# Two contraction blocks in three split passes, sums with a guard column, and value products one block of work later

## The chip, the cores and the metric

The kernel runs on one core of one Trainium2 chip. The metric is device time in microseconds (us); the median of three runs of the kernel before is 1055.7 us (1055.4 to 1057.94). The engines that matter are PE (matrix products), ACT and DVE (elementwise work, also out of the matrix product's banks), POOL (elementwise work between tiles in SBUF, and some of the transfers) and SP, whose queue starts most transfers.

## What is computed

Chunked attention feeds a first gated layer, and that feeds a second one. Attention has 4 batches, 8 heads, 768 positions and a head size of 64. The keys of a chunk of 32 positions are 8 memory keys, 16 to its left, its own 32 and 8 to its right.

```python
def _attn_ref(q, k, v, mem_k, mem_v) -> np.ndarray:
...
    for c in range(nc):
...
        scores = scale * np.matmul(q_c, k_full.transpose(0, 1, 3, 2))
        scores = scores - np.max(scores, axis=-1, keepdims=True)
        a = np.exp(scores)
        a = a / (np.sum(a, axis=-1, keepdims=True) + 1e-09)
        out[:, :, c_start:c_end] = np.matmul(a, v_full)

def _moe_ref(x, w1, w2, w3, w_out) -> np.ndarray:
    a = x @ w1
    b = x @ w2
    h = a * b @ w3
    return (h @ w_out).astype(np.float32)

def _moe2_ref(x, w_a, w_b, w_out) -> np.ndarray:
    a = x @ w_a
    b = x @ w_b
    return (a * b @ w_out).astype(np.float32)
```

There are 3072 tokens of width 512. The inner width is 1024 in the first layer and 1536 in the second.

## The kernel before

**Order.** The kernel is written under a manual schedule: each engine, and each queue of transfers, takes its instructions in the order in which the program issues them. So the place of a call in the Python loops is its place on the engine.

**The weights' product.** Since `h @ w_out` is `(a * b) @ (w3 @ w_out)`, the kernel first makes the product of `w3` and `w_out` once. This is the tile `wps` (loop at L576 of the profile): two halves, in each half eight contraction blocks k, in each block four banks m, so 64 products of 128 x 128 by 128 x 512 in full fp32. The profile lists each of these as two PE records. A number `g = 2k + m // 2` counts 16 places in a half. Behind a place come one "slot" of attention and, at listed places, `w_tick()`, which moves a three-step pipeline of weight loads by one (scaling on ACT at L403 and L404, joining of the halves of a word on DVE at L409, splitting into high and low parts on ACT and DVE). When the eighth block of a bank is done, `w_evict` (L571) takes it out of its bank: a high part on ACT (L573), and a low part on DVE.

**Split products.** All later matrix products are made from split factors. ACT rounds a factor to fp32r (the high part, `split_hi`, L104), DVE subtracts it from the factor (the low part, `split_lo`, L107), and three passes are summed in one bank: high by high, high by low, low by high.

**Attention.** It is done in 16 units, u = 0 to 15, each with two groups of 96 query rows and 4 head pairs. The stages of a unit are: `a_k`, `a_q`, `a_v` (transfers of keys, queries, values, on SP's queue), `a_scores` (tile `sc`, 96 small products on PE), `a_max` (largest score, and its subtraction, on DVE), `a_exp` (ACT), `a_norm` for each half of the heads (sum, plus 1e-9, reciprocal and multiplication; DVE, and the multiplication of u < 6 on POOL), `a_trans` (tile `pt`, 8 transposes on PE), `a_pt` (copy of `pt` to `p2` on ACT), `a_pv` (tile `xp`, 96 small products with the values on PE) and `a_x` (`xp` into the token tile `xt`, or, for the last two token tiles, over `xo` to DRAM, `xd`). `pt` and `xp` share one pair of banks (tag `px`), and `p2` and `xo` share one buffer (tag `p2`, one buffer).

Each stage has a slot: `BASE[u]` plus an offset, for u > 2 the offsets 8 (transposes and `p2`), 11 (value product and the next unit's values) and 12 (`a_x`); the next unit but one begins 14 slots behind `BASE[u]`, since units lie 7 slots apart. `between()` (L702) is called twice in each step of the first layer, once behind `psA` and once behind `psB` (12 split products of 128 x 512 each), and runs as many slots as a pace needs that is worked out from `NEED`, the slot by which a token tile has to be there.

**Layers.** Token tiles 0 to 3 go through `psA`, `psB` (gate) and `psY` (product with the weights' product) while attention runs beside them. Tiles 4 and 5 and the second layer go through a scheme of seven block products (`ps`, `ops`), which the change doesn't touch.

The pieces of code that matter here, as the profile numbers them:

## Time and profile before

| | us |
|---|---|
| median of the runs | 1055.7 (1055.4 to 1057.94) |
| profiled execution | 1054.13 |
| its span in the trace | 1052.3 |
| PE busy | 1045.2 |
| DVE, ACT, POOL busy | 595.1, 446.5, 250.4 |

The span is what the trace sees from the first to the last instruction; 1.8 us of the profiled execution lie outside it. The granted clock of PE is 1.00 in every slice. A PE row of the timeline is drawn somewhat longer than the distance to the next row's start (records overlap in the pipeline), so the price of a group on PE is read as the distance from its start to the start of what follows.

### The profile page before, as it was taken

The numbers are of one execution on the slowest core, as the hardware profiler recorded it, in microseconds if no ns is written. First come the engines' busy times: TensorE is split into PE (matmuls) and PEld (weight loads), VectorE is DVE, ScalarE is ACT, GpSimd is POOL, SyncE is SP. The second block draws the span as 40 slices with busy tenths as digits, with TensorE's granted clock in tenths as the row PEclk, the third lists the DMA queues.
The fourth block names the chain that finished last, engine by engine and source line by source line (L and its number), as shares of the span: only waits on it lengthen the run. The fifth ranks groups of instructions, "written<-read, shape, count | busy, mean of one in ns | idle before, by whom it ended". The sixth has DMA issues, their size and how long they took to land.

```text
span 1052.3 us, 18316 instructions
## 1 busy us (share of the span) xinstructions
PE 1045.2 (99%) x7394; PEld 835.9 (79%) x7394; DVE 595.1 (57%) x950; ACT 446.5 (42%) x797; POOL 250.4 (24%) x264
## 2 busy tenths in 40 slices
PE   9999999999999999999999999999999999999998
PEld 3458788888888888888888888888888888888886
DVE  5889946766775437257666656554444454444410
ACT  5666623434544434344654445333434334343310
POOL 0102498132222000000133334012232202322210
PEclk9999999999999999999999999999999999999999
DMA  9986567678886333144533332344332323222211
GB/s 331 322 218 196 147 200 261 202 243 285 293 275 189 113 101 101 70 132 130 188 111 116 137 133 70 121 143 153 135 130 71 115 76 111 70 70 71 71 40 40
DMA packets 77301, 157.35 MB, mean 150 GB/s; under 512 B 8224, under 2 KB 38304, under 8 KB 75936
## 3 DMA queue, kind: packets, MB, share of 16 engines
q1 hardware_dynamic: 68944, 123.10, 35.5%
q0 software_dynamic: 8064, 33.03, 9.5%
q8 instruction: 58, 0.95, 0.4%
q14 instruction: 27, 0.22, 0.1%
q10 hardware_dynamic: 208, 0.04, 0.0%
HBM read 118.92 MB, written 37.22 MB: 148 GB/s over the span
## 4 chain that ended last, share of the span: by engine, by line
PE 91%; DMA 4%; DVE 2%; ACT 1%; issue 1%; SPq 0%; DVEq 0%; ACTq 0%
PE ps L913 40%; PE ops L95 19%; PE psY L95 11%; PE psB L95 7%; PE psA L95 7%; PE wps L95 3%; PE xp L95 2%; DMA raw<-in_w3a 2%; PE sc L95 1%; DMA raw<-in_w 1%; PE pt L233 1%; DMA q<-in_qt 1%; DVE dec L409 0%; DMA xb<-yd 0%; ACT raw L403 0%
## 5 line engine op out<-in xcount | busy, mean ns | idle before, releaser
L913 PE MATMUL ps<-x,w 128*128 128x512 f32 x1848 | 425.5, 389 | 0.2 <-ACT tmp L925 0.2
L913 PEld LDWEIGHTS ps<-x,w 128*128 128x128 f32 x1848 | 346.6, 188 | 73.2 <-ACT tmp L925 1.1
L925 ACT ACTIVATE tmp<-ps 128x512 f32<-128x512 f32 x132 | 78.6, 596 | 267.5 <-PE ps L913 245.4
L107 DVE TENSOR_TENSOR w<-w 128x512 fp32r<-128x512 f32 (+1 forms) x176 | 108.0, 631 | 79.7 <-ACT w L104 79.5
L1085 DVE TENSOR_TENSOR tmp<-ps,tmp 128x512 f32<-128x512 f32 x108 | 74.6, 691 | 130.0 <-PE ps L913 96.3
L95 PE MATMUL psY<-g,wo 128*128 128x512 f32 x576 | 134.5, 391 | 0.0
L95 PEld LDWEIGHTS psY<-g,wo 128*128 128x128 f32 x576 | 107.4, 188 | 22.4
L1098 POOL TENSOR_TENSOR g<-tmp,g 128x512 fp32r<-128x512 f32 x66 | 88.8, 1360 | 150.3 <-ACT g L104 150.3
L95 PE MATMUL ops<-wo,g 128*128 128x512 f32 x504 | 118.6, 389 | 0.0
L95 PEld LDWEIGHTS ops<-wo,g 128*128 128x128 f32 x504 | 94.6, 188 | 19.6
L804 POOL DMA_DIRECT2D w<-wc x36 | 20.0, 557 | 354.6 <-PE ps L913 216.5
L95 PE MATMUL psA<-xt,w 128*128 128x512 f32 x384 | 94.5, 395 | 0.3 <-ACT xt L104 0.3
L95 PE MATMUL psB<-xt,w 128*128 128x512 f32 x384 | 93.8, 393 | 0.0
L104 ACT ACTIVATE w<-w 128x512 fp32r<-128x512 f32 (+1 forms) x176 | 92.1, 572 | 1.9 <-DMA w<-wd 1.9
L95 PEld LDWEIGHTS psA<-xt,w 128*128 128x128 f32 x384 | 70.8, 188 | 16.1 <-ACT xt L104 1.1
L95 PEld LDWEIGHTS psB<-xt,w 128*128 128x128 f32 x384 | 71.2, 188 | 15.0
L95 PE MATMUL ops<-fo,g 128*128 128x512 f32 x288 | 68.2, 389 | 0.0
L403 ACT ACTIVATE raw<-raw 128x512 f32<-128x512 f32 (+1 forms) x66 | 49.0, 743 | 33.2 <-DMA raw<-in_wab 17.9
L95 PEld LDWEIGHTS ops<-fo,g 128*128 128x128 f32 x288 | 54.1, 188 | 11.2
L95 PE MATMUL wps<-w_f 128*128 128x512 f32 x128 | 57.6, 599 | 0.7 <-DVE w_f L409 0.7
L104 ACT ACTIVATE g<-tmp 128x512 fp32r<-128x512 f32 x82 | 47.2, 624 | 19.1 <-DVE tmp L929 11.1
L404 ACT ACTIVATE raw<-raw 128x512 uint32<-128x512 uint32 (+1 forms) x66 | 49.0, 742 | 0.0
(73 smaller groups left out, 933.7 us busy)
## 6 DMA issues: line engine op xcount, KB each, us to landing
w<-wc POOLq DMA_DIRECT2D x36, 640.0 KB, 4.2
raw<-in_wab SPq DMA_DIRECT2D x24, 512.0 KB
v<-in_vw SPq DMA_DIRECT2D x64, 168.0 KB
w<-wc POOLq DMA_DIRECT2D x36, 256.0 KB, 3.7
kraw<-in_kt SPq DMA_DIRECT2D x16, 512.0 KB
raw<-in_w3a SPq DMA_DIRECT2D x6, 1024.0 KB
q<-in_qt SPq DMA_DIRECT2D x16, 384.0 KB
wc<-cs SPq DMA_DIRECT2D x12, 512.0 KB
```

What stands on the lines that cost most here:

```text
L95: nc.tensor.matmul(o, lhsT=l, rhs=r, start=first, stop=last)
L104: nc.scalar.activation(hi, src, AF.Copy)
L107: nc.vector.tensor_tensor(lo, src, hi.bitcast(F32), ALU.subtract)
L233: nc.tensor.transpose(pt[:, a // 4, a % 4, :], t[:, a].rearrange("p r k -> p (r k)"), id_sb)
L403: nc.scalar.activation(h, h, AF.Prelu, scale=2.0**-112, alpha=2.0**32)
L404: nc.scalar.activation(l, l, AF.Copy, scale=2.0**-29)
L804: (nc.gpsimd if c else nc.sync).dma_start(out=t[:, 1, :C7].bitcast(F32), in_=wseq[n][:, :C7])
L913: nc.tensor.matmul(ps, lhsT=w[i][:, a, k, :], rhs=xs[i][:, b, k, :], start=first and n == 0, stop=n == 5, skip_group_check=not first,)
L925: nc.scalar.activation(z, ps, AF.Copy)
L1085: nc.vector.tensor_tensor(z, ps, y, ALU.add)
L1098: nc.gpsimd.tensor_tensor(g[:, 1, :], z, g[:, 0, :].bitcast(F32), ALU.subtract)
```

## The change

There are four parts.

1. In the second half of the weights' product the blocks k = 6 and 7 are made from split factors: `w_split` rounds the two factors of a block on ACT and takes the low parts on POOL, and `w_mm` issues three passes in place of one full fp32 product. The new tiles lie in a pool of weight loads whose work is then over (tag `raw2`, three buffers). The turns of `w_tick` at g = 13 and 14 of this half move to 12 and 13.
2. The tile `t` of a unit's exponentials becomes one of two persistent tiles `tt`. A head pair's 128 columns lie there in rows of 129, with a column of 1e-9 at each border, set once by POOL. One reduction over 65 elements (64 keys and a guard column) and one reciprocal per unit replace two reductions, two additions and two reciprocals. The multiplication runs on POOL for u = 0 alone, and otherwise on DVE.
3. From u = 4 on the slots of a unit are 9 (transposes and `p2`), 14 (value product, next values) and 15 (`a_x`) in place of 8, 11 and 12, and `NEED` is 3 slots later.
4. The first keys and queries (`a_k(0)`, `a_q(0)`) are called at g = 2 and 3 of the first half, and no longer at g = 0.

```diff
@@ -35,6 +35,7 @@
 KD = DM // P
 M1 = DF1 // P
 M2 = DF2 // P
+KR = 2 * KEYS + 1
 NEG = -1.0e30
 CH = 512
 BUFS = {"raw64": (3, 0), "raw2": (0, 3), "dec": (4, 3)}
@@ -98,6 +99,7 @@
     ks, qs, scs, soft, pts, p2s, xps = ({} for _ in range(7))
     v = att.tile([P, NE, NC, 4 * D], F32, tag="v", bufs=1, name="v")
     kw = att.tile([P, NH, NC, KEYS], F32, tag="kw", bufs=1, name="kw")
+    tt = [att.tile([GQ, NH * KR + 1], F32, tag="t", bufs=2, name="tt") for _ in range(2)]
     xt = {}
 
     def split_hi(hi, src):
@@ -182,6 +184,11 @@
         m = mask_sb[rs, None, None, 0 : c1 - c0].to_broadcast([CHUNK, 2, 4, c1 - c0])
         nc.vector.tensor_tensor(x, x, m, ALU.add)
 
+    def with_eps(u):
+        t = tt[u % 2]
+        p, x = t.ap
+        return bass.AP(t.tensor, t.offset, [p, [KR * x[0], NH], [(KEYS + 1) * x[0], 2], [x[0], KEYS + 1]])
+
     def a_max(u):
         sc = scs.pop(u)
         for e in range(NE):
@@ -191,7 +198,8 @@
                 a_edge(sc, slice(0, CHUNK), hs, NMEM, NMEM + LEFT)
             if g == NG - 1:
                 a_edge(sc, slice(GQ - CHUNK, GQ), hs, KEYS - RIGHT, KEYS)
-        t = att.tile([GQ, NH, 2, KEYS], F32, tag="t", bufs=2, name="t")
+        t = tt[u % 2][:, : NH * KR].rearrange("p (a x) -> p a x", x=KR)[:, :, 1:]
+        t = t.rearrange("p a (r k) -> p a r k", r=2)
         mx = att.tile([GQ, 2, NH], F32, tag="mx", bufs=2, name="mx")
         sm = att.tile([GQ, NH, 2], F32, tag="sm", bufs=2, name="sm")
         nc.vector.tensor_reduce(mx, sc, axis=mybir.AxisListType.X, op=ALU.max)
@@ -215,11 +223,11 @@
     def a_norm(e):
         def stage_of(u):
             t, mx, sm = soft[u][1:]
+            if e == 0:
+                nc.vector.tensor_reduce(sm, with_eps(u), axis=mybir.AxisListType.X, op=ALU.add)
+                nc.vector.reciprocal(sm, sm)
             t, sm = t[:, 4 * e : 4 * e + 4], sm[:, 4 * e : 4 * e + 4]
-            nc.vector.tensor_reduce(sm, t, axis=mybir.AxisListType.X, op=ALU.add)
-            nc.vector.tensor_scalar_add(sm, sm, 1e-9)
-            nc.vector.reciprocal(sm, sm)
-            (nc.gpsimd if u < 6 else nc.vector).tensor_tensor(
+            (nc.gpsimd if u < 1 else nc.vector).tensor_tensor(
                 t, t, sm[:, :, :, None].to_broadcast([GQ, 4, 2, KEYS]), ALU.mult
             )
 
@@ -292,7 +300,7 @@
         todo.setdefault(s, []).extend(stages)
 
     for u in range(NA):
-        t0, t1, t2, t3 = SLOTS.get(u, (8, 8, 11, 12))
+        t0, t1, t2, t3 = SLOTS.get(u, (8, 8, 11, 12) if u < 4 else (9, 9, 14, 15))
         for s, stage_of in (
             (t0, a_trans),
             (t1, a_pt),
@@ -318,7 +326,7 @@
     NEED = []
     for i in range(NT1):
         u = -(-TT * (i + 1) // (NE * GQ)) - 1
-        NEED.append(BASE[u] + (13 if u > 2 else 10))
+        NEED.append(BASE[u] + (16 if u >= 4 else 13 if u > 2 else 10))
     acount = [0]
 
     held_back = []
@@ -555,8 +563,13 @@
 
     w_load()
     warm = psd.tile([P, 512], F32, tag="d", name="warm")
-    wz = att.tile([GQ, 2, TT], F32, tag="t", bufs=2, name="wz")[:, 0]
+    wz = att.tile([GQ, NE, 4, GQ], F32, tag="p2", bufs=1, name="wz")
+    wz = wz.rearrange("p e a q -> p (e a q)")[:, :TT]
     nc.vector.memset(wz, 0.0)
+    for i in range(2):
+        p, x = tt[i].ap
+        eps = bass.AP(tt[i].tensor, tt[i].offset, [p, [KR * x[0], NH + 1]])
+        nc.gpsimd.memset(eps, 1e-9)
     for _ in range(5):
         mm(warm[:GQ], wz[:, :GQ], wz, True, True)
     w_load()
@@ -573,17 +586,32 @@
         nc.scalar.activation(w[:, 0, :], banks[m], AF.Copy)
         nc.vector.tensor_tensor(w[:, 1, :], banks[m], w[:, 0, :].bitcast(F32), ALU.subtract)
 
+    S3 = (6, 7)
+    w_hl = {}
+
+    def w_split(i):
+        k, j = S3[i // 2], i % 2
+        if k not in w_hl:
+            w_hl[k] = p0.tile([P, 4, CH], F32R, tag="raw2", bufs=3, name="w_hl")
+        x = w3k[8 + k] if j else wo_f[k]
+        h, l = w_hl[k][:, 2 * j], w_hl[k][:, 2 * j + 1]
+        nc.scalar.activation(h, x.bitcast(F32), AF.Copy)
+        nc.gpsimd.tensor_tensor(l, x.bitcast(F32), h.bitcast(F32), ALU.subtract)
+        (wo_f, w3k)[j][(k, 8 + k)[j]] = (h, l)
+
+    def w_mm(o, k, kk, m):
+        a, b = w3k[kk], wo_f[k]
+        if not isinstance(a, tuple):
+            mm(o, a.bitcast(F32)[:, P * m : P * m + P], b.bitcast(F32), k == 0, k == 7)
+            return
+        for i, (p, q) in enumerate(PASSES):
+            mm(o, a[p][:, P * m : P * m + P], b[q], k == 0 and i == 0, k == 7 and i == 2)
+
     for half in range(2):
         banks = [psd.tile([P, 512], F32, tag="d", name="wps") for _ in range(4)]
         for k in range(8):
             for m in range(4):
-                mm(
-                    banks[m],
-                    w3k[8 * half + k].bitcast(F32)[:, P * m : P * m + P],
-                    wo_f[k].bitcast(F32),
-                    k == 0,
-                    k == 7,
-                )
+                w_mm(banks[m], k, 8 * half + k, m)
                 if k == 7 and m > 0:
                     w_evict(half, m - 1)
                 if m % 2 == 0:
@@ -594,8 +622,9 @@
                         attn_slot()
                     if g in (0, 2, 4, 6, 8, 9):
                         w_tick()
-                    if g == 0:
+                    if g == 2:
                         a_k(0)
+                    if g == 3:
                         a_q(0)
                     if g == 7:
                         a_keys(0)
@@ -606,9 +635,12 @@
                         w_turn()
                 else:
                     attn_slot()
+                    for i in range(2 * len(S3)):
+                        if (2, 6, 3, 7, 7, 8, 11, 12)[i] == g:
+                            w_split(i)
                     if g == 0:
                         w_next()
-                    if g in (1, 4, 5, 6, 9, 10, 13, 14):
+                    if g in (1, 4, 5, 6, 9, 10, 12, 13):
                         w_tick()
         w_evict(half, 3)
     del pairs["f"]
```

On PE, in a stretch of the first layer with tiles of later units, the value product of a unit stands by itself before (`psA` and `psB` are the two gate products of a step, `w_...` its weights, `sc` the scores, `pt` the transposes):

```order
L95 MATMUL xp<-p_1884,v 64x32 x48
L95 MATMUL psA<-xt,w_869 128x512 x12
L95 MATMUL psB<-xt,w_869 128x512 x12
L95 MATMUL sc<-kw,q 32x64 x48
L95 MATMUL psA<-xt,w_934 128x512 x12
L233 MATMUL pt<-id_sb,t 128x96 x8
L95 MATMUL psB<-xt,w_934 128x512 x12
```

and in the changed kernel, in the same steps:

```order
L96 MATMUL psA<-xt,w_884 128x512 x12
L96 MATMUL xp<-p_1887,v 64x32 x48
L96 MATMUL sc<-kw,q 32x64 x48
L96 MATMUL psB<-xt,w_884 128x512 x12
L96 MATMUL psA<-xt,w_947 128x512 x12
L241 MATMUL pt<-id_sb,tt 128x96 x8
L96 MATMUL psB<-xt,w_947 128x512 x12
```

The value product now stands directly ahead of the scores of the unit after the next, so that two groups of small products lie in one gap between the large ones instead of two. This is so ten times (value products of u = 4 to 13).

On ACT, in the last blocks of the weights' product's second half (`raw_...` is the scaling of a landed weight block, `p_...` the copy of u = 2's transposes, `w_...` a high part, `wo` the eviction of a bank of the weights' product, `xt` the high part of the first token tile), before:

```order
L445 ACTIVATE w_657<-dec 128x512
L403 ACTIVATE raw_579<-raw_579 128x512
L404 ACTIVATE raw_579<-raw_579 128x512
L239 ACTIVATE p_695<-pt 128x768
L445 ACTIVATE w_699<-dec 128x512
L403 ACTIVATE raw_664<-raw_664 128x512
L404 ACTIVATE raw_664<-raw_664 128x512
L573 ACTIVATE wo<-wps 128x512
L445 ACTIVATE w_699<-dec 128x512
L403 ACTIVATE raw_677<-raw_677 128x512
L404 ACTIVATE raw_677<-raw_677 128x512
L573 ACTIVATE wo<-wps 128x512 x2
```

and in the changed kernel:

```order
L453 ACTIVATE w_656<-dec 128x512
L411 ACTIVATE raw_581<-raw_581 128x512
L412 ACTIVATE raw_581<-raw_581 128x512
L453 ACTIVATE w_697<-dec 128x512
L411 ACTIVATE raw_663<-raw_663 128x512
L412 ACTIVATE raw_663<-raw_663 128x512
L247 ACTIVATE p_712<-pt 128x768
L453 ACTIVATE w_697<-dec 128x512
L411 ACTIVATE raw_676<-raw_676 128x512
L412 ACTIVATE raw_676<-raw_676 128x512
L586 ACTIVATE wo<-wps 128x512 x3
```

The copy of the transposes now stands behind the scaling of one more weight block (raw_663, the block that was raw_664), and the first eviction behind both blocks.

On SP's queue of transfers at the start (`raw_...` are weight blocks, `kraw` and `q` the first keys and queries), before:

```order
L388 DMA raw_154<-in_w3a 128x2048
L388 DMA raw_167<-in_w3a 128x2048
L123 DMA kraw<-in_kt 128x2x512
L130 DMA q<-in_qt 128x2x384
L388 DMA raw_181<-in_w3a 128x2048
L388 DMA raw_192<-in_w3a 128x2048
```

and in the changed kernel:

```order
L396 DMA raw_158<-in_w3a 128x2048
L396 DMA raw_171<-in_w3a 128x2048
L396 DMA raw_181<-in_w3a 128x2048
L125 DMA kraw<-in_kt 128x2x512
L132 DMA q<-in_qt 128x2x384
L396 DMA raw_196<-in_w3a 128x2048
```

The seventh weight block now goes ahead of the first keys and queries.

## Rows read from the trace of the kernel before

**Rows 1.** The page, part 1: busy us, share of span, instructions.

```profile
PE 1045.2 (99%) x7394; PEld 835.9 (79%) x7394; DVE 595.1 (57%) x950; ACT 446.5 (42%) x797; POOL 250.4 (24%) x264
```

**Rows 2.** Waits of PE: us in total, times, longest us.

```profile
PE wps L95 <- DVE w_f L409: 0.7, 2, 0.5
PE psA L95 <- ACT xt L104: 0.3, 1, 0.3
PE pt L233 <- DVE xt L107: 0.3, 1, 0.3
```

**Rows 3.** Chain that ended last, in order of time: start us, us, what.

```profile
18.04 8.89 DMA raw<-in_w3a
30.95 9.16 DMA q<-in_qt
41.44 5.35 PE wps L95 x12
```

**Rows 4.** Timeline of PE, 163 to 185: start, us, what [wait <- releaser].

```profile
163.88 2.88 PE L95 MATMUL psA<-xt,w 128*128 128x512 f32 x12
166.60 2.88 PE L95 MATMUL psB<-xt,w 128*128 128x512 f32 x12
169.41 1.60 PE L95 MATMUL xp<-p,v 64*64 64x32 f32 x96
170.95 3.02 PE L95 MATMUL psA<-xt,w 128*128 128x512 f32 x12
173.80 2.88 PE L95 MATMUL psB<-xt,w 128*128 128x512 f32 x12
176.62 1.20 PE L95 MATMUL sc<-kw,q 64*32 64x64 f32 x96
177.74 3.02 PE L95 MATMUL psA<-xt,w 128*128 128x512 f32 x12
180.60 0.82 PE L233 MATMUL pt<-id_sb,t 96*128 96x96 f32 x8
181.21 3.01 PE L95 MATMUL psB<-xt,w 128*128 128x512 f32 x12
```

**Rows 5.** Timeline of PE, 219 to 232, scores directly ahead of transposes.

```profile
219.69 1.20 PE L95 MATMUL sc<-kw,q 64*32 64x64 f32 x96
220.81 0.88 PE L233 MATMUL pt<-id_sb,t 96*128 96x96 f32 x8
221.48 8.45 PE L95 MATMUL psY<-g,wo 128*128 128x512 f32 x36
229.85 1.60 PE L95 MATMUL xp<-p,v 64*64 64x32 f32 x96
```

**Rows 6.** Windows: PE, PEld, DVE, ACT, POOL busy, clock, DMA share, GB/s.

```profile
64.00:70.00 6.00, 6.00 (x28) 3.08 (x22) 5.57 (x9) 2.58 (x4) 0.20 (x1) 1.00 0.86 210
```

**Rows 7.** Timelines of ACT and PE, 70 to 80, end of the weights' product.

```profile
70.18 0.81 ACT L239 ACTIVATE p<-pt 128x768 f32<-128x768 f32 x1 [3.31 <-PE pt L233]
...
76.17 0.60 ACT L573 ACTIVATE wo<-wps 128x512 fp32r<-128x512 f32 x1 [0.69 <-PE wps L95]
...
73.48 1.60 PE L95 MATMUL xp<-p,v 64*64 64x32 f32 x96
...
77.31 3.02 PE L95 MATMUL psA<-xt,w 128*128 128x512 f32 x12 [0.32 <-ACT xt L104]
```

**Rows 8.** Source lines on DVE: shortest/median/longest ns, first and last us.

```profile
L220 DVE TENSOR_SCALAR sm<-sm x32: 167/168/4394, 36.0 to 336.3; 96x8 f32<-96x8 f32 x32
L222 DVE TENSOR_TENSOR t<-t,sm x20: 686/689/1498, 143.8 to 337.0; 96x512 f32<-96x512 f32 x20
```

**Rows 9.** Source line on POOL with the size of the new subtractions.

```profile
L649 POOL TENSOR_TENSOR g<-gv,g x8: 1278/1289/1607, 89.8 to 137.3; 128x512 fp32r<-128x512 f32 x8
```

**Rows 10.** Timelines of PE and ACT, 313 to 325, u = 13.

```profile
313.27 1.60 PE L95 MATMUL xp<-p,v 64*64 64x32 f32 x96
...
321.87 0.60 ACT L273 ACTIVATE xo<-xp 128x512 f32<-128x512 f32 x1 [6.46 <-DMA xd<-xo]
```

## The prediction

> **What bounds the kernel now.** I read the busy times first: PE is busy for 99% of the span and no other engine for more than 57% [rows 1]. Then the waits of PE: behind the warm-up the three largest are 0.7 us before blocks of the weights' product, 0.3 us before the first gate product, and 0.3 us before one group of transposes [rows 2]. So a gain can come from four places only: PE work that is taken away, the gaps that PE pays when it goes from one sort of product to another, those three waits, and the start, where the chain of waits still runs through transfers, the longest being 8.89 us for a weight block and 9.16 us for the second unit's queries [rows 3]. Everything else that the change takes off DVE or POOL is worth nothing by itself. The profiled execution took 1054.13 us with a span of 1052.3; the median of the runs is 1.6 us above it. I make the sum on the profiled execution and carry it over to the median 1055.7. A measurement of this kernel can tell about 0.3%, 3.2 us, from no change.
>
> **Three passes.** A stretch of the weights' product lists 12 records, six full products, in 5.35 us [rows 3]. A row outlasts the start of the next by 0.16 (2.88 long, next start 2.72 later [rows 4]), so one full product costs (5.35 − 0.16) / 6 = 0.86 us. Twelve products of split factors, of the same size, take 166.60 − 163.88 = 2.72 us [rows 4], 0.227 each, three of them 0.68. That saves 0.18 on each of 8 products: **−1.4 us**. The eight new instructions on ACT and POOL stand at g = 2 to 7, long before the blocks that need them at g = 12 and 14. POOL was busy for 0.2 us of the 6 from 64 us on, ACT for 2.6 [rows 6]. Four subtractions of POOL at 1.29 each [rows 9] and four copies of ACT at 0.6 [rows 7] fit in, and cost nothing while that cover lasts. DVE in that window is busy for 5.57 of 6 us [rows 6], but gets none of them.
>
> **What is late next there.** The first gate product already waits 0.32 us for the token tile's high part, which ACT does behind the eviction that starts at 76.17, itself waiting for PE [rows 7]. The last two banks become shorter by 0.18 each, and the eviction chain with its 0.6 us copies does not: I give back **+0.3**, nothing at best and 0.7 at worst. There is a second point: the copy of u = 2's transposes now stands behind the scaling of one more weight block. Before it started at 70.18, released by PE alone [rows 7]. The transfers ran at 210 GB/s in the six microseconds to 70 [rows 6], some 1.26 MB, and what SP has queued up to this block (values, four of 56x3x256 words, 0.69 MB; the block before it, 128x4x256 words, 0.52 MB) is about that, so I estimate a landing at 69.9, the two scalings (0.6 each) done at 71.1 and the copy at 71.9. The value product was started at 73.48 [rows 7] and will be wanted six saved products earlier, at 72.4. The slack is 0.5 us: cost nothing, but little cover.
>
> **The wait before one group of transposes** (0.3 us [rows 2]) was DVE being late with a low part. DVE loses two additions of 0.17 a unit, of which one lasted 4.39 us [rows 8] with DVE standing behind POOL's multiplication, and some of the reductions. It gets two multiplications of 0.69 [rows 8] in each of u = 1 to 5. That is +0.9 us of plain work a unit, less the stalls. I take the wait as gone, **−0.3**, with 0 and −0.3 as ends.
>
> **Fewer gaps on PE.** Where a group of small products stands alone, the large ones around it cost more. Ahead of the value product 12 products take 169.41 − 166.60 = 2.81, behind it 173.80 − 170.95 = 2.85, against 2.72: 0.09 and 0.13. For the scores it is 176.62 − 173.80 = 2.82 and 180.60 − 177.74 = 2.86: 0.10 and 0.14 [rows 4]. So a group by itself costs 0.23. What two small groups cost between them is seen at one place: scores directly ahead of transposes take 220.81 − 219.69 = 1.12, as alone (177.74 − 176.62), and the transposes 221.48 − 220.81 = 0.67 in place of 181.21 − 180.60 = 0.61 [rows 4, 5]. So the second group costs 0.06 and not 0.23: 0.17 saved. The change puts value products directly ahead of scores ten times, and takes that one neighbourhood of scores and transposes apart: 10 × 0.17 − 0.17 = **−1.5 us**. The ends are −0.7, if the edge between the two costs as much as one beside a large group, so that a pair saves 0.09 and not 0.17, and −2.1, if it costs nothing (10 × 0.23 − 0.17).
>
> [...]
>
> **What the later slots delay.** The token tile's `a_x` comes 3 slots later, which `NEED` allows for; the copies of transposes and `xo` share one buffer and the transposes and the value product one pair of banks. This matters at u = 13, whose tokens fall into two tiles, so that it copies out twice. The second copy waits 6.46 us for the first one's transfer and starts at 321.87, 7.0 us behind the value product's end (313.27 + 1.60); it ends after 0.60 [rows 10], 7.6 behind. The next transposes need that bank. Now they are wanted after the scores and two blocks of 12, 1.12 + 2.86 + 2.81 = 6.8 us behind. PE stands for **+0.8 us**, between 0 (the transfer is issued sooner) and 2.5 (it is issued behind the next values on SP's queue and takes a third longer).
>
> **The start.** The seventh weight block goes ahead of the first keys and queries. The waits before the weights' product's blocks (0.7 us [rows 2]) should go, but the queries and keys come some 1 MB later on queues that are full, and the second unit's queries, for which PE now waits at the end of 9.16 us [rows 3], bring PE back to the same point. I take **−0.1 us**, from −0.5 (both waits gone) to +0.4 (the first scores wait).
>
> **Sum.** −1.4 + 0.3 − 0.3 − 1.5 + 0.8 − 0.1 = −2.2 us: 1051.9 in the profiled execution, **1053.5** against the median, 0.2% faster. With each term at its better end: −1.4 − 0.3 − 2.1 − 0.5 = −4.3. With each at its worse: −1.4 + 0.7 − 0.7 + 2.5 + 0.4 = +1.5.
>
> **Rivals.**
> 1. *The passes are eaten at the hand-over.* If the weight block lands at 71.2 or later, 1.3 us behind my estimate, the copy of transposes ends at 73.2, the value product starts 0.8 late and the rest of the evictions stack up behind it; then the 1.4 us of the passes are returned, and −1.1 is left: 1054.6. For it: DVE is full there, and the longest transfer at the start took 9 us [rows 3, 6]. Against it: ACT had been idle for 3.31 us at this place [rows 7].
> [...]
> 3. *All covers hold.* The second `xo` is in time, the start gives 0.5 and a pair saves the full 0.23: −3.3 to −4.3, some 1051.8. For it: `xo`'s stall is a single case of 0.8 us out of a wait of 6.46. Against it: it needs three terms at their better ends at once.
> 4. *Slower: the one buffer of `p2` and `xo` becomes the bound.* For u = 10 to 15 `xo` goes out one slot ahead of the next unit's copy `p2`, where three slots lay between. `p2` then stands on ACT until `xo`'s transfer has landed, some 6.46 − 2.8 = 3.7 us, and the copies out of the gate's banks are queued behind it. There are four such banks, so PE is covered for about two blocks, 5.7 us; it decides from a transfer of 8.5 us on. At 9.5 PE waits 1 us at each of five units, and u = 13 costs 3.8 in place of 0.8: −3.0 + 5 + 3.8 = +5.8, 1061.5. For it: the next values (four transfers, eight at a new batch) are queued ahead on the same queue. Against it: the one measured wait, 6.46 us [rows 10], lies 2 us below the point.
> 5. *The subtractions on POOL hold DVE up.* DVE is full at 64 to 70 us [rows 6], and DVE's small additions have stood 4.39 us beside POOL's work [rows 8]. Four times 1.29 us [rows 9] are 5.2 us of DVE; it has 7% of idle time there, 1.5 us in the twenty ahead of 70, so that the last weights come up to 3.7 us later. Half of that on PE gives 1055.4, within 0.3%. [...]
>
> **How the numbers follow.** Forecast (−0.9 to −3.1) 0.50; rival 1 0.12; rival 2 0.08, most of it inside the forecast's own band; rival 3 0.20; rival 4 0.06; rival 5 0.04. Faster by over 0.3% is rival 3 almost whole and the far end of the forecast, 0.28. Slower by over 0.3% is rival 4 and a little of others: 0.07. The rest is within 0.3%: 0.65. The range leaves out rival 4's far part and the best end of rival 3: 1051.2 to 1056.2.
>
> **What would show it.** The products of k = 6 and 7 of the second half at 0.227 us a pass, and the first gate product waiting between 0.5 and 0.8 us behind ACT. Value products directly ahead of scores, with 2.81 us for the 12 products before the pair and 2.86 for those behind, and some 0.06 more for the pair than the 1.54 and 1.12 us of the two alone. PE's waits: `pt` behind ACT's `xo` once, near 320 us, 0.8 us; no wait for a low part near 120. I am wrong if PE waits for the copy `p2` near 72 us (rival 1), if the joined groups show a second gap of 0.1 or more (rival 2), if `psA` or `psB` waits for ACT at several units from 250 us on (rival 4), or if DVE's rows between 50 and 65 us are long beside POOL's (rival 5).

## The result and the profile after

The changed kernel takes 1063.98 us in the median (1059.62 to 1068.26, 6 runs), the kernel before 1055.55 in the median of its 6. The ratio is 1.0081, with a 95% interval of 1.0064 to 1.0097: slower by 0.8%, where 0.2% faster was forecast, and outside the forecast's range. The profiled execution took 1063.89 us, its span is 1062.1.

The busy time of PE is what it was [rows 1]: it went down by 0.6 us while the span grew by 9.8. So PE stands still more. The page of the changed kernel, part 1 and two rows of part 2:

```profile
PE 1044.6 (98%) x7402; PEld 840.5 (79%) x7402; DVE 581.9 (55%) x896; ACT 449.1 (42%) x801; POOL 247.9 (23%) x260
...
PE   9899999999899999999999999999999999999998
...
PEclk9999999999899999999999999999999999999999
```

In the slice at 266 to 292 us PE is no longer full and the granted clock is lower than elsewhere. The waits of PE say what it stood for (us in total, times, longest), to be held against [rows 2]:

```profile
PE sc L96 <- issue: 7.2, 3, 3.8
PE sc L96 <- DVE kw L163: 1.8, 1, 1.8
...
PE sc L96 <- DMA q<-in_qt: 1.3, 1, 1.3
PE psY L96 <- issue: 0.6, 1, 0.6
PE xp L96 <- ACT p L247: 0.5, 1, 0.5
PE psA L96 <- ACT xt L106: 0.5, 1, 0.5
```

The first line is new in kind. "Issue" is time in which the engine waits for nothing that the profile shows: no semaphore, no transfer, no other engine. The timeline of PE shows where (start, us, what, and in brackets the wait):

```profile
254.42 1.60 PE L96 MATMUL xp<-p,v 64*64 64x32 f32 x96
255.95 0.95 PE L96 MATMUL sc<-kw,q 64*32 64x64 f32 x71
258.76 0.46 PE L96 MATMUL sc<-kw,q 64*32 64x64 f32 x25 [1.85 <-issue]
...
276.42 1.60 PE L96 MATMUL xp<-p,v 64*64 64x32 f32 x96
277.96 0.79 PE L96 MATMUL sc<-kw,q 64*32 64x64 f32 x54
282.54 1.07 PE L96 MATMUL sc<-kw,q 64*32 64x64 f32 x42 [3.80 <-issue]
283.54 5.16 PE L96 MATMUL psB<-xt,w 128*128 128x512 f32 x12
288.53 2.92 PE L96 MATMUL psA<-xt,w 128*128 128x512 f32 x12
```

PE stops in the middle of a group: the first 71, or 54, of the 96 small products of the scores run, the rest 1.85 or 3.80 us later. Their operands are the same tiles, so a missing operand is unlikely. It happens four times, always inside or just behind the scores that follow a value product directly: behind record 88 at 237 us (1.57), 71 at 259 (1.85), 54 at 283 (3.80), and behind 9 products of `psY` after the scores at 217 (0.57), 7.8 us in all. The step between these places is 17 records each time. Windows around the longest one (columns as in [rows 6]):

```profile
276.00:278.70 2.70, 2.70 (x153) 2.19 (x151) 2.29 (x5) 2.00 (x4) 0.79 (x1) 1.00 0.38 53
278.80:282.50 3.70, 0.00 (x0) 0.00 (x0) 0.00 (x0) 0.86 (x2) 2.35 (x4) 0.84 1.03 401
282.60:288.50 5.90, 5.90 (x54) 4.71 (x55) 0.00 (x0) 0.00 (x0) 0.00 (x0) 0.53 0.71 177
288.60:291.00 2.40, 2.40 (x12) 1.97 (x11) 2.16 (x3) 0.00 (x0) 0.00 (x0) 1.00 1.24 360
```

After 3.7 us without work the granted clock is 0.53 for the next 5.9 us. The 12 products of `psB` take 288.53 − 283.54 = 4.99 in place of 2.86, the last 42 scores 1.00 in place of 0.49: 2.6 us more for one stop.

### The profile page after: what moved, and what is told of

Read it like the earlier page. It is cut to its first block, busy times and chain, and to the rows that moved or that the text cites. A ratio compares the mean times of both kernels' runs of the same rounds, so it can differ in the third digit from the quotient of the medians.

```text
span 1062.1 us, 18273 instructions
## 1 busy us (share of the span) xinstructions
PE 1044.6 (98%) x7402; PEld 840.5 (79%) x7402; DVE 581.9 (55%) x896; ACT 449.1 (42%) x801; POOL 247.9 (23%) x260
## 4 chain that ended last, share of the span: by engine, by line
PE 92%; DMA 3%; ACT 2%; DVE 2%; issue 1%; SPq 0%; ACTq 0%; DVEq 0%
PE ps L945 39%; PE ops L96 18%; PE psY L96 12%; PE psB L96 9%; PE psA L96 8%; PE xp L96 2%; PE sc L96 2%; DMA raw<-in_w3a 1%; PE pt L241 1%; DMA kraw<-in_kt 1%; PE wps L96 1%; ACT raw L411 1%; DMA raw<-in_w3b 1%; ACT raw L412 1%; DVE w_f L417 0%
## 5 line engine op out<-in xcount | busy, mean ns | idle before, releaser
L96 PE MATMUL psB<-xt,w 128*128 128x512 f32 x384 | 96.5, 401 | 0.0
L411 ACT ACTIVATE raw<-raw 128x512 f32<-128x512 f32 (+1 forms) x66 | 48.9, 740 | 22.8 <-DMA raw<-in_w3a 11.4
L96 PE MATMUL wps<-w_f 128*128 128x512 f32 x112 | 49.8, 597 | 0.0
L678 DVE TENSOR_TENSOR gv<-psB,gv 128x512 f32<-128x512 f32 x32 | 22.0, 686 | 50.0 <-PE psB L96 48.4
```

The costliest lines, as they stand in the source:

```text
L96: nc.tensor.matmul(o, lhsT=l, rhs=r, start=first, stop=last)
L411: nc.scalar.activation(h, h, AF.Prelu, scale=2.0**-112, alpha=2.0**32)
L678: nc.vector.tensor_tensor(gv, psB[:, :TT], gv, ALU.mult)
```

## A theory, and the runs that test it

**Theory.** The page of the changed kernel, part 3, has a queue for instructions (packets, MB, share of 16 engines):

```profile
q8 instruction: 58, 0.95, 0.4%
```

PE has 7402 products and as many weight loads, 14804 instructions; if this queue is PE's, a packet holds 255 of them (256 with PE's 71 semaphore and drain instructions) and 16 KB. One such block is 128 records of products with their weight loads. A border between blocks therefore comes every 128 records, whatever they cost: 29 us in large products at 0.227, but 1.7 us in the small ones. Two groups of 96 in a row hold 192 records, so two borders can fall into them, and the second block has to arrive in 1.7 to 1.8 us. At 259 us the border is behind record 71 of the scores, the one before it 128 records earlier, behind 39 of the value product; 57 × 0.016 + 71 × 0.0117 = 1.74 us lie between, and with the wait of 1.85 the block took 3.6. From one pair to the next PE issues 272 records in most units, 16 past two blocks, which is about the shift of 17.

The trace bears this out in two more ways. Count every PE instruction ahead of the record at which PE goes on: two for each record, and the semaphore and drain instructions. Ahead of the four stops stand 5313, 5825, 6337 and 6849, so from stop to stop it is 512, two blocks to the instruction. And just before PE goes on a packet of the instruction queue has landed: at 215.73, 235.40, 257.53 and 281.19 us, 1.70, 1.47, 1.22 and 1.35 us ahead. The same holds for all 37 such stops, of this run and of those below: 192 or 193 instructions past a multiple of 256, and a packet landed 1.2 to 1.7 us before.

**Rivals.** The stops come from the new softmax (part 2); from a buffer or transfer at these places; or only from the values of the next unit, whose transfers start just there.

Each experiment's columns and lines are as above. "Stretch" is the time from the first gate product (first `psA`) to the first product of the seven-product scheme (first `ps`). It is 311.98 us in the kernel before (77.31 to 389.29) and 320.27 in the changed one (78.43 to 398.70); it leaves out the start, which differs between profiled executions: the first gate product comes at 75.50 to 79.48 us. The ends of the stretch, before (its start is in [rows 7]) and then in the changed kernel:

```profile
389.29 1.98 PE L913 MATMUL ps<-x,w 128*128 128x512 f32 x8
...
78.43 3.01 PE L96 MATMUL psA<-xt,w 128*128 128x512 f32 x12 [0.48 <-ACT xt L106]
...
398.70 1.52 PE L945 MATMUL ps<-x,w 128*128 128x512 f32 x6
```

**Part 3 undone.**

```diff
-        t0, t1, t2, t3 = SLOTS.get(u, (8, 8, 11, 12) if u < 4 else (9, 9, 14, 15))
+        t0, t1, t2, t3 = SLOTS.get(u, (8, 8, 11, 12))
...
-        NEED.append(BASE[u] + (16 if u >= 4 else 13 if u > 2 else 10))
+        NEED.append(BASE[u] + (13 if u > 2 else 10))
```

> The changed kernel with part 3 alone undone: slots 8, 8, 11, 12 and NEED as in the kernel before; three passes, guard sums and the later first keys and queries stay. Theory (instruction blocks: PE's instructions come in blocks of 256, that is 128 records with their weight loads, and two groups of 96 small products in a row use up more than one block in the time that the next needs to arrive): no PE wait put down to issue is left, the slice at 250 to 300 us is back at a granted clock of 1.00, and the time falls by 7.8 us of issue waits and about 2.4 us at half clock, less the joined groups' gain of 1.5: 1055 to 1057. Rival (the waits come from DVE's or POOL's new work on the softmax, so from part 2): the issue waits stay near 220 to 283 us, and the time stays above 1061.

Measured: 1052.93 us (ratio to the kernel before 0.9979, 0.9968 to 0.9989), no wait for issue, a granted clock of 1.00, a stretch of 311.15. The time is lower than the 1055 to 1057 expected. So the whole loss, and more, sits in part 3; the softmax is not its cause.

**All borders moved by 64 records.**

```diff
         mm(warm[:GQ], wz[:, :GQ], wz, True, True)
+    for _ in range(32):
+        mm(warm[:CHUNK, :CHUNK], wz[:, :CHUNK], wz[:, :CHUNK], True, True)
```

> The changed kernel with 32 small fp32 products (64 records on PE) added behind the warm-up, while PE has nothing else to do before the first weights land; all else the same. Theory (blocks of 128 records, counted from the program's start): every block border comes 64 records earlier in the later program. The waits behind record 88, 71 and 54 of the scores and behind 9 products of psY vanish at these places (217, 237, 259 and 283 us), and waits may show where a border now falls into the last part of a joined pair with another border inside its value products: scores of the pairs near 152, 172 and 192 us (about records 90, 73 and 57), and near 303 and 324 us. The size there depends on the transfers at that time. Rival (the waits hang on a transfer, a buffer or a semaphore at these places): they stay where they are, at the same records, 7 to 8 us in all.

Measured: 1069.4 us (1.013, 1.011 to 1.015). The timeline of PE, every row with a wait for issue:

```profile
158.56 0.31 PE L96 MATMUL sc<-kw,q 64*32 64x64 f32 x1 [4.24 <-issue]
...
182.89 0.42 PE L96 MATMUL sc<-kw,q 64*32 64x64 f32 x19 [1.41 <-issue]
...
204.94 0.63 PE L96 MATMUL sc<-kw,q 64*32 64x64 f32 x36 [2.03 <-issue]
...
309.49 4.97 PE L96 MATMUL psY<-g,wo 128*128 128x512 f32 x21 [1.78 <-issue]
...
329.93 0.38 PE L96 MATMUL sc<-kw,q 64*32 64x64 f32 x14 [1.35 <-issue]
```

With 1, 19 and 36 records left of 96, the stops are behind record 95, 77 and 60 in the pairs where 90, 73 and 57 were foretold, and none is left at the four old places. Nothing about those pairs had changed but the count of instructions ahead of them. This settles that the borders of instruction blocks set the places. The forecast's miss of 3 to 5 records goes away when PE's semaphore instructions are counted too: the five stops stand behind 3777, 4288, 4801, 7616 and 8128 instructions, each 192 or 193 past a multiple of 256.

**Values two slots later.**

```diff
-            (t2, lambda u: a_v(u + 1)),
+            (t2 + (2 if u >= 4 else 0), lambda u: a_v(u + 1)),
```

> The changed kernel with the next unit's values (a_v) issued two slots later for u from 4 on, so that their transfers no longer run while PE is in the scores behind the value product. Theory A (the block comes late because the value transfers stand ahead of it in the DMA engines): the issue waits of 0.57, 1.57, 1.85 and 3.80 us shrink to under 1.5 in sum, and the time comes to 1054 to 1057. Theory B (a block takes its 3 us whatever else is moved): the waits stay, 5 us or more in sum, 1060 or more.

Measured: 1066.45 us (1.0103, 1.0082 to 1.0124), waits for issue of 9.7 us in sum, 2 or 3 records behind the old places (behind 90, 73 and 57 of the scores, and one more behind 31 at 153 us); PE has 3 to 6 semaphore instructions fewer ahead of them here, and the count ahead of each stop is again 192 or 193 past a multiple of 256. So the values' transfers are not the cause.

**Part 4 undone.**

```diff
-                    if g == 2:
+                    if g == 0:
                         a_k(0)
-                    if g == 3:
                         a_q(0)
```

> The changed kernel with part 4 alone undone: first keys and queries at g = 0 of the first half. Theory: the first scores wait no more for the keys (1.78 us at 28 us) and the second ones for little of the 1.33 us at 42; small waits for weight blocks come back (0.24 and 0.46 in the kernel before). The first gate product starts 1 to 1.7 us earlier than 78.43. The issue waits near 217 to 283 us stay at the same records, about 7 us in sum, since the order on PE is the same. Time 1061 to 1063. Rival (the hand-over at 70 to 78 us is what costs, whatever the start): the first gate product stays within 0.3 us of 78.4.

Measured: 1064.62 us (1.0089, 1.0065 to 1.0112), above the 1061 to 1063 expected, the stops at the same records (8.2 us in sum). The first scores no longer wait, and the first gate product starts at 77.20. But PE still waits there, 0.8 us for the copy `p2` and 0.7 for the token tile.

**Parts 1 and 2 alone** (both edits above together).

> Parts 1 and 2 alone (three passes, guard sums, multiplication on DVE from u = 1 on): slots and first keys and queries as before. Theory (part 4 costs 1.2 us at the start, since the first gate product came at 78.43 with it and at 77.20 without): first gate product near 77.2, a wait of the value product for the copy p2 of about 0.8 us and one of the first gate product of 0.7 still there, time 1051.5 to 1053.0. Rival (the start comes out alike either way, transfers being full): same as with slots alone undone, within 0.5 us of it.

Measured: 1053.38 us (0.9987, 0.9977 to 0.9997), first gate product at 76.76, waits of 0.72 and 0.65 there, stretch 311.14. The time is a little above the 1051.5 to 1053.0 of the theory and within 0.5 us of the run with part 4 kept, as the rival had it. Against the run with part 4 kept (0.9979) no difference can be seen in the time, so the price of part 4, about 1 us in the traces, stays unproved.

**Turns of the weights' pipeline back,** on parts 1 and 2 alone.

```diff
-                    if g in (1, 4, 5, 6, 9, 10, 12, 13):
+                    if g in (1, 4, 5, 6, 9, 10, 13, 14):
```

> As parts 1 and 2 alone, with the turns of the weights' pipeline back at g = 13 and 14, so that the copy of u = 2's transposes stands on ACT ahead of the scaling of the block of weights that landed last. Theory (the 1.4 us of the passes are eaten by ACT's order at 70 to 77 us): no wait of the value product for p2, first gate product near 76.3, 0.8 to 1.1 us less than parts 1 and 2 alone. Rival (ACT has too much to do there in any order): the wait moves to the first gate product, which stays within 0.3 us.

Measured: 1053.38 us (0.9982, 0.9974 to 0.9991). The copy is not waited for any more. From the second scores to the first gate product it takes 77.72 − 41.84 = 35.88 us, where the kernel before took 37.06 (40.25 to 77.31), the changed one 36.44 (41.99 to 78.43), and parts 1 and 2 alone 36.94 (39.82 to 76.76). By these traces the order on ACT would cost 0.6 to 1.1 us of the three passes' gain. Six other runs below have the same program up to there: they take 36.08 to 36.84 us, and their first gate product waits 0.57 to 1.22 us for ACT. The seven runs with the turns moved take 36.44 to 37.16. The medians are 36.26 and 36.66, so the order costs about 0.4 us, in ranges that overlap, and part of the wait moves to the first gate product, as the rival had it. The forecast of 76.3 us for that product was missed (77.72), and in the time the effect is too small to be seen.

**Transposes ahead of scores**, in place of value products ahead of scores (slots 7, 7, 11, 12 from u = 4 on, on the run with the turns back).

```diff
-        t0, t1, t2, t3 = SLOTS.get(u, (8, 8, 11, 12))
+        t0, t1, t2, t3 = SLOTS.get(u, (8, 8, 11, 12) if u < 4 else (7, 7, 11, 12))
```

> As the one with the turns back, and from u = 4 on the transposes one slot earlier, so that they stand directly ahead of the next unit's scores: 104 small records in a row, fewer than one block, where value products and scores were 192. Theory (blocks of 128 records): no wait put down to issue; each of eleven pairs saves some 0.17 us, less one such neighbourhood that is there anyway: 1.5 to 1.7 us less than without it. Rival (any joined pair of small groups costs waits, or transposes wait for the softmax one slot earlier): waits of transposes for DVE or of scores for issue, and no gain.

Measured: 1058.71 us (1.0034, 1.0022 to 1.0046). No wait for issue, as foretold for 104 records, but the waits of PE have new lines:

```profile
PE pt L241 <- DVE xt L109: 3.2, 1, 3.2
...
PE pt L241 <- ACT xo L281: 0.9, 1, 0.9
```

At u = 4 the transposes come one slot behind the eviction of u = 3's value product, whose banks they need, and again the clock falls behind the idle time (0.73 over 6.3 us). Against the run with the turns back (1053.38) it loses some 5 us where 1.5 to 1.7 of gain were expected. The rival's reason was right, not the theory's gain.

**Part 3 alone on the kernel before** (the first diff of this section, the other way round, in the old kernel).

> The kernel before with part 3 alone (slots 9, 9, 14, 15 and NEED). Theory: PE has 8 records fewer before the first gate product than the changed kernel, so the borders fall 8 records later: issue waits behind about record 96, 79 and 62 of the scores and behind 17 products of psY, near 216 to 282 us, 6 to 10 us in all with the slow clock: 1060 to 1066. Rival (it takes the softmax of part 2 as well): no such waits and 1053 to 1055.

Measured: 1068.35 us (1.0125, 1.0108 to 1.0142), with waits for issue of 9.1 us in sum: 3.53, 2.85 and 1.41 behind record 94, 77 and 60 (foretold 96, 79, 62), and 1.27 behind 54 at 136 us; at 217 us, where one was foretold too, there is none, and the time is above the 1060 to 1066 expected. The eight records that PE has fewer here, less three semaphore instructions more, move the places by 6.

**Joined only for u = 5, 6, 7 and 13,** the others at 8, 8, 11, 12 (parts 1 and 2 with the turns back; only the edit of the slots is shown).

```diff
+    JOIN = (5, 6, 7, 13)
...
+        t0, t1, t2, t3 = SLOTS.get(u, (9, 9, 14, 15) if u in JOIN else (8, 8, 11, 12))
```

> Parts 1 and 2 with the turns back at g = 13 and 14, and value products joined with scores (slots 9, 9, 14, 15) only for u = 5, 6, 7 and 13, where by the count of PE's records no two block borders fall into a pair's 192 records close together; the other units keep 8, 8, 11, 12. Theory (blocks): no wait put down to issue, and each of the four pairs saves 0.23 us: 0.9 us less than without them. Rival (any joined pair costs): issue waits at 150 to 195 or near 323 us, and a slower kernel.

Measured: 1060.88 us (1.0058, 1.0044 to 1.0071). No wait for issue, yet slower: where a unit at slots 14 and 15 is followed by one at 8, the transposes stand next to `a_x` and wait for it, 0.87 and 1.81 us for DVE and 2.56 for `xo`. The runs with transposes at 9 for all units, below, take this away.

**Products of 128x32 in the quieter stages.**

```diff
+        if i == 0 and calls[0] in (3, 6, 10, 16, 22, 28, 34, 40):
+            for _ in range(192):
+                mm(
+                    ps[:CHUNK, :CHUNK],
+                    w[0][:, 0, 0, :CHUNK].bitcast(F32),
+                    xs[0][:, 0, 0, :CHUNK].bitcast(F32),
+                    True,
+                    True,
+                )
```

> Parts 1 and 2 with the turns back, and at eight places of the later stages (seven-product scheme and second layer, where the transfers are lighter) 192 small products, 384 records, put ahead of a product into the same bank, which that product then overwrites. It adds PE work; its time is not to be compared. Each place holds three block borders 128 records apart. Theory A (a block takes 3 to 6 us to come only where the transfers are heavy): with 384 records at 12 to 16 ns, some 1.5 to 2 us between borders, waits of under 0.5 us a border where the DMA share is 0.2, and more where it is 0.5. Theory B (a block takes its 3 us anywhere): a wait of 1 to 2 us at each second and third border, whatever the share.

Measured: no wait at any border. But these 384 records took 12.35 us, 4.1 for 128, so this says only that a block came within 4.1 us there.

**Fewer other transfers.**

```diff
-                if wdone[0]:
-                    cw_step()
-                else:
+                if not wdone[0]:
                     next(dw, None)
```

> The changed kernel with the conversion of the second layer's weights (transfers of 0.5 MB in, and their results out, that run beside attention from about 190 us on) left for the stages behind attention. The order on PE is the same. Theory A (the blocks are late because of the other transfers in the DMA engines): the issue waits at 217 to 283 us, 7.8 us before, fall below 3 us. Theory B (a block takes its time anyway): they stay, 6 us or more. The time of the whole may be worse for what is late afterwards; the waits are what counts.

Measured: the DMA share falls from 0.77 to 0.30 at 200 to 250 us, and the stops stay at the same records, 1.70, 1.55 and 1.34 us, 4.6 in sum against 7.2, and without the one at `psY`. Both numbers of the expectation are missed: less than 6 and more than 3. With the time between the borders (1.67, 1.74, 1.81) a block takes 3.1 to 3.4 us here, and 3.2, 3.6 and 5.6 beside the full traffic. So most of it is the block's own time, and the traffic adds up to 2.5 us at one of the three. The packets show where: each starts 0.63 to 0.84 us behind the border here, and 0.70, 1.55 and 3.49 us behind it beside the full traffic.

**Joined for u = 5, 6, 7 and 13, the rest one slot earlier** (transposes at 9 for all, value products at 13; turns and first keys as before; u = 14 and 15 have no scores behind them to join).

```diff
+    JOIN = (5, 6, 7, 13, 14, 15)
...
+        ... else (9, 9, 14, 15) if u in JOIN else (9, 9, 13, 14)
```

> The changed kernel's slots (transposes at 9) with first keys and queries and the weights' turns as before, and value products at 14, joined with scores, only for u = 5, 6, 7 and 13; for u = 4 and 8 to 12 the value product stands one slot earlier (13), so that a block of large products lies between it and the scores. The transposes keep their distance from the slot of a_x, so none has to wait for it as where slots 8 and 9 were mixed. Theory (blocks): no wait put down to issue, no transposes behind DVE or xo; the stretch from the first gate product to the first product of the seven-product scheme, 311.0 us with no pair joined, becomes 0.9 us shorter, 310.1, and the whole 1052 to 1053. Rival (joining gains nothing): 311 us or more in that stretch.

Measured: 1053.96 us (0.9981, 0.9972 to 0.9991), and two waits for issue are left, behind the old records 88 and 71 (0.53 and 0.75), though 12 large products lie between the groups. The border before lies in the value product, 28 and 45 records from its end; 45 × 0.016 + 2.95 + 0.83 = 4.5 us, and the block took 5.2. The stretch is 311.72 where 310.1 was expected, and the time is above the 1052 to 1053 expected.

**Products of 64x32 in the quieter stages**, at the same eight places.

```diff
+            for j in range(192):
+                c, r = j % 4, 0
+                mm(
+                    ps[CHUNK * c : CHUNK * c + CHUNK, D * r : D * r + D],
+                    w[0][rows(r), 0, 0, :CHUNK].bitcast(F32),
+                    xs[0][rows(r), 0, 0, :D].bitcast(F32),
...
```

> Parts 1 and 2 with the turns back, and at the same eight places of the later stages 192 products (384 records) of the tile size of the scores (64x32) put ahead of a product into the same bank, over four column groups in turn, so that 128 records take less than 4.1 us. It adds PE work; its time is not to be compared. Theory A (a block comes in well under 3 us where the transfers are light): no wait put down to issue where 128 records take 2 us or more. Theory B (a block takes some 3.2 us by itself, as the waits with fewer transfers suggest: 1.67 + 1.70, 1.75 + 1.55, 1.81 + 1.34): at each place two waits of 1 to 1.5 us, such that the time from one border to the next is 3 to 3.4 us.

Measured, at the first place, where the DMA share is 0.21:

```profile
404.30 3.44 PE L96 MATMUL ps<-x,w 64*32 64x64 f32 x231
409.83 2.74 PE L96 MATMUL ps<-x,w 64*32 64x64 f32 x128 [2.10 <-issue]
413.56 0.90 PE L96 MATMUL ps<-x,w 64*32 64x64 f32 x25 [0.99 <-issue]
```

Here a block is seen whole: 128 records from one stop to the next, and 413.56 − 409.83 = 3.7 us from border to arrival. There is a stop at each of the eight places, ten in all, 18.2 us in sum. With the border before put 256 instructions ahead of the stop, the ten blocks took 3.3 to 5.1 us, eight of them 3.3 to 4.1, at DMA shares of 0.08 to 0.38. So a block takes some 3.7 us (their median) far from attention and its transfers too: theory B in kind, though it foretold two waits at each place and 3 to 3.4 us.

**Joined for the same four, the rest two slots earlier** (value products at 12).

```diff
-        ... else (9, 9, 14, 15) if u in JOIN else (9, 9, 13, 14)
+        ... else (9, 9, 14, 15) if u in JOIN else (9, 9, 12, 13)
```

> As the run before with joined pairs for u = 5, 6, 7 and 13, and for u = 4 and 8 to 12 the value product one slot earlier still (12), so that two blocks of large products, 5.5 us, lie between it and the scores. Theory (a block of 256 instructions takes up to 5.9 us, as the longest wait showed; one block of large products gave it 4.3 to 4.4, and it waited 0.53 and 0.75): no wait put down to issue is left, and the stretch from the first gate product to the first product of the seven-product scheme comes to 310.0 to 310.4 us, against 311.0 with no pair joined. Rival (the waits come with the later slots, not with the spacing): waits of 0.5 us or more at the same records.

Measured: 1052.44 us, the kernel before 1055.92 in the same job: 0.997 (0.9959 to 0.998). No wait for issue. The stretch is 387.77 − 77.58 = 310.19, in the foretold band, against 311.03 with no pair joined: 0.21 a pair, from one execution of each. In the times the gain of joining is not separate from noise (0.9959 to 0.998 against 0.9974 to 0.9991 with no pair joined).

```profile
151.44 1.60 PE L96 MATMUL xp<-p,v 64*64 64x32 f32 x96
152.97 1.19 PE L96 MATMUL sc<-kw,q 64*32 64x64 f32 x96
154.09 3.02 PE L96 MATMUL psY<-g,wo 128*128 128x512 f32 x12
156.95 2.89 PE L96 MATMUL psA<-xt,w 128*128 128x512 f32 x12
...
387.77 1.52 PE L945 MATMUL ps<-x,w 128*128 128x512 f32 x6
```

This kernel is faster than both. The runs with parts 1 and 2 are faster than before as well, by 0.1 to 0.2%.

## Why the prediction was wrong, step by step

**Fewer gaps on PE: the step that failed.** The sum priced a pair by its edges alone, and took it that PE issues 192 small products one after the other. The edges came out at the better end: in the lines above the value product takes 1.53 and the scores 1.12, with 2.86 behind, so nothing is lost between the two groups and a pair saves its full 0.23, −2.1 us in all. The second gap of 0.1 or more in the joined groups (rival 2) is not there: scores behind value products cost what they cost alone, 1.12 [rows 4]. But 7.8 us of stops and 2.6 us at the lower clock came with it, +10.4 where the worse end of the term was −0.7. The trace of before had the number that was needed: 14788 PE instructions in 58 packets. It showed no such stop, since no two small groups of 96 stood together there; scores and transposes [rows 5] are 104 records, less than a block, and were no fair model for 192.

**Three passes.** The size was right: 8 products at three passes. In the run with the turns back, 12 passes between the transposes (done at 71.12) and the value product (74.04) take 2.92 us, and 2.70 without the two edges: 0.225 a pass. But rival 1 was half true. ACT in the changed kernel:

```profile
72.77 0.69 ACT L411 ACTIVATE raw<-raw 128x512 f32<-128x512 f32 x1 [1.33 <-DMA raw<-in_w]
73.36 0.67 ACT L412 ACTIVATE raw<-raw 128x512 uint32<-128x512 uint32 x1
73.92 0.79 ACT L247 ACTIVATE p<-pt 128x768 f32<-128x768 f32 x1
```

ACT stands 1.33 us for the weight block, which lands near 72.7 and not at 69.9, and the copy behind it ends at 74.7; the value product waits 0.50 for it. The first gate product waits 0.48 in place of 0.32, +0.2 where +0.3 was given back. From the second scores on −0.6 is left of the −1.1 forecast, and −1.2 in the run with the order on ACT put back; in the medians of seven runs each it is −0.4 and −0.8.

**The wait before one group of transposes** (0.3) is gone, as forecast. The new softmax gave more than that: the stretch is 0.84 us shorter with parts 1 and 2 and no change of slots (311.98 to 311.14), and this wait, read from start to start, is 0.48 of it. DVE is busy 13 us less, where +0.9 us of plain work a unit was worked out. The additions are gone, which took 13.3 us in sum and not 32 × 0.17; the reciprocals take 2.4 us less, the reductions (half as many, each about twice as long) 1.8 less, and the multiplications 5.5 more.

**Later slots.** The second `xo` waits 5.34 us for the first one's transfer and starts at 330.42; the transposes start at 331.17 without a wait. The term was +0.8 and is 0, by little: the second `xo` ends at 331.02, 0.15 us ahead of the transposes, and with part 3 alone they waited 0.53 us for it. Rival 4 did not come either, no gate product waits for ACT in that part.

**The start.** The term was −0.1 with +0.4 as its worse end; in the profiled execution the first scores wait 1.78 us for the keys and the second ones 1.33 for the queries, and the second scores start at 41.99 in place of 40.25: +1.7. The five executions with part 4 gave 40.5 to 42.5, the eleven without it 38.7 to 41.9, with medians of 41.99 and 40.88. So some 1 us may be part 4's, but the ranges overlap, and the rest is the start's own spread.

**The subtractions on POOL** (rival 5) took 1.28 us each, between 51 and 65 us, and no PE wait for DVE's weights is left at that time: they were hidden. Beside them the rows of DVE run at most 0.16 us over the median of their form (0.84 for 0.69 at 65.73, 0.83 for 0.69 at 57.51). Before, nine of the 32 small additions lasted 0.33 to 4.39 us, and each of the nine ended 0.02 to 0.03 us behind the end of a POOL operation. The one of 4.39, from 128.03 to 132.42, stood beside four of them: the multiplication that the prediction names ended at 128.65, the last of the other three at 132.40.

**The sum by measured terms,** against the profiled execution of before: start +1.7, hand-over −0.6, stretch +8.3, the rest +0.4, which is 9.8 us. In the stretch, stops +7.8, lower clock +2.6, softmax −0.8 and pairs −2.1 make +7.5, 0.8 short. The waits as listed leave that out: read from start to start, as the prices of groups are, the four stops cost 0.88, 1.81, 2.08 and 4.46 us and the twelve products behind the last one 2.13, 11.4 in all, and the sum comes to +8.5. The other executions lie between 1059.6 and 1068.3; that the length of the stops changes from one to the next is likely, but only one execution has a trace.

**What stays open.** A block took 2.9 to 6.1 us from one border to PE's going on at the next, over the 37 stops (read from start to start, which gives 0.1 to 0.2 more than the waits as listed). The packet itself took 0.9 to 1.6 us and PE went on 1.2 to 1.7 us after it had landed; what differs most is when the packet starts, 0.4 to 3.7 us behind the border. In the changed kernel the pairs at 134 and 303 us have two borders as close as the others (1.77 and 1.82 us) and didn't wait: there the packet had started 1.05 and 2.87 us ahead of the first border. With part 3 alone the pair at 134 us waited 1.27. What decides when the packet starts wasn't found, beyond the share of the traffic seen above.

## What to carry to other kernels

Before groups of very short products are put side by side, count PE's instructions: here 128 products with their weight loads filled a block of 256, and runs of 192 small ones stopped for their own instructions at four of ten places, for 0.57 to 3.80 us. The stop of 3.80 us cost 2.6 us more at the lower clock. Keep large products between such groups (here one block of 12 still left stops of 0.53 and 0.75 us, two blocks left none), or join them only where the count from the program's start puts no two borders close together. And if a change that saves edges on the bounding engine makes it slower, look for "issue" in its waits before anything else.

## What the runs showed of the hardware

- PE's instructions came in packets of 16 KB, 256 instructions; where 128 records lasted less than the block took to come, PE stopped in the middle of a group, 0.4 to 4.2 us at a time. All 37 stops lie 192 or 193 instructions past a multiple of 256, and end 1.2 to 1.7 us after a packet has landed. A block took 3.3 to 5.1 us in the two runs with lighter transfers (DMA share 0.08 to 0.38), with a median of 3.7 in the added products, and 2.9 to 6.1 beside the full traffic (about 0.8).
- After the stop of 3.80 us the granted clock was 0.53 over 5.9 us; after the stops of 1.57 and 1.85 us in the same trace the next twelve products took 2.88 and 2.86, full speed. In other runs they took 4.44 after a stop of 1.70 (fewer transfers, granted clock 0.97 over 200 to 250 us) and after one of 1.85 (part 4 undone), and 3.83 to 5.29 after the other eight of 2.03 to 4.24 ahead of large products.
- Value products (64x64) directly ahead of scores (64x32) lost nothing between them: 1.53 and 1.12 us, as apart.
